# Turning the second product of a fused attention and GELU feed-forward kernel: w_out as the weights, the GELU halves as the moving side

## The chip, the cores and the metric

The kernel runs on one core of a Trainium2 chip. The metric is the device time of one execution in microseconds, as the median of repeated runs; less is better.

## What is computed

A gated linear attention (4 sequences, 8 heads, 768 steps, head size 48) whose output, 3,072 tokens by 384 columns, goes through a feed-forward layer with GELU:

```python
for t in range(S):
    state = alpha[:, :, t, :, None] * state + np.einsum('bhd,bhe->bhde', k[:, :, t], v[:, :, t])
    y[:, :, t] = np.einsum('bhd,bhde->bhe', q[:, :, t], state)
x = y.transpose(0, 2, 1, 3).reshape(B * S, H * D)          # 3072 x 384
h = x @ w_in                                               # 384 x 2048
g = 0.5 * h * (1.0 + erf(h * inv_sqrt2))
return (g @ w_out).astype(np.float32)                      # 2048 x 384
```

## The kernel before

**Work and tiles.** The tokens are cut into 12 groups of 256 (G), the 2,048 inner columns into 8 pairs of 128 (f). Both products are made of three matmuls in place of one: each operand is split into a high and a low half, and high x high, high x low and low x high are added in PSUM. A *step* is one pair of g and f, and there are 96.

**First product** (`gemm1`, L565 to L579). For each of the two blocks of a pair and each of three blocks of 128 rows it runs three matmuls: weights are a 128 x 128 block of w_in (`wih`, `wih`, `wil`), the moving side is 256 tokens of x (high, low, high). That is 18 matmuls of 256 columns into a tile `hp` of 512 columns.

**GELU.** ACT reads `hp` twice (L592, L593): once to a rounded high half `ghi`, once in place. DVE subtracts to the low half `glo` (L598). Each half is a tile of 2 x 256 columns, and two of each take turns.

**Second product** (`gemm2`, L614 to L624). For each of two blocks of 128 tokens the weights are a 128 x 128 block of a GELU half, and the moving side is a 384-column row block of w_out (`woh`, `wol`). Eight matmuls take `ghi`, then four take `glo`: 12 of 384 columns into two accumulators of 128 x 384, each in a PSUM bank of its own. The accumulators are kept while a group goes on through f, and then copied out (`evacuate`, L630 to L644): added to or copied into the tile `part` by DVE (L634, L638) or ACT (L636), the accumulators one after the other. When all of w_out has been added, POOL issues the DMA that stores `part` (L644); for the last group SP and ACT issue one DMA for each half (L640).

**Order.** A planner lays all work out before it is written down, with a table of costs (`COST`) and rules of readiness, and the order on PE, DVE, ACT and SP is then fixed by hand. After a group's x is ready PE alternates between first and second product; the second product of a step comes after the first product of the next. In between PE makes *visits* to the attention part: small tiles of 64 x 64 and 48 x 64 (L398, L425, L324, L486). In 18 visits of the later part a memset on POOL (L833, the *fence*) stands between the two halves of a visit: it waits for the matmuls before it, and the matmuls of L486 wait for it. It goes through the same queue as the output's DMA of L644.

**Places in SBUF.** Tiles are laid one behind another in their pools. `X_GAP`, `HI_GAP` and `LO_GAP` (L35) put unused bytes ahead of some tiles. With them all weight tiles begin 32 bytes past a multiple of 256, the x tiles 224 bytes past one, and the GELU halves 32 bytes past one.

Of the kernel before, what the change touches and what calls it, by code (L numbers as in the profile page):

```python
# [8 lines left out]
F32 = mybir.dt.float32  # L9
# [6 lines left out]
ALU = mybir.AluOpType  # L16
# [15 lines left out]
RATE, ALONE, LATENCY, SMALL, BEGIN = 350e3, 290e3, 2.1, 50e3, 2.2  # L32
MARGIN = 1.5
HOME = {0: 0, 1: 1, 2: 2, 4: 1, 5: 0, 6: 2, 8: 1, 9: 0, 10: 2, "s": 1}
X_GAP, Z_GAP, HI_GAP, LO_GAP, LATE_GAP = (128, 0, 192), 0, (64, 0), (0, 64), 0  # L35
COST = dict(
    scan=0.65, back=0.72, keys=0.65, q=1.35, qv=0.62, scores=1.0, kn=0.5, mask=0.62, inside=1.05, chain=1.15, outer=0.85, carry=0.26, last=0.34, last_p=0.15, sums=0.55, scaled=0.45,
    xh=0.6, xl=0.65, spread=0.62, check=0.95, load=0.46, fetch=0.46, u=0.92, c0=0.56, c1=0.9, c2=0.45, c3=0.95, c4=0.92,
# [6 lines left out]
def gla_then_gelu_ffn(ctx: ExitStack, tc: tile.TileContext, q, k, v, alpha, akq, w_in, w_out, out):  # L45
    nc = tc.nc
    B, H, D, S = q.shape
    NF, P, NK, _ = w_in.shape
    DM, DFF = NK * P, NF * P
    NT = B * S  # L50
    C = 128
    G = 2 * C
# [8 lines left out]
    NG = B * GPB  # L61
    NSB = GPB
# [4 lines left out]
    const = ctx.enter_context(tc.tile_pool(name="const", bufs=1))  # L67
# [5 lines left out]
    ps_o = ctx.enter_context(tc.tile_pool(name="ps_o", bufs=1, space=PSUM))  # L73
# [429 lines left out]
    def x_tiles(g):  # L503
        if g != "s" and g % (XB + 1) == XB:
            x = late[0].tile([P, NK, 2, G], F32R, tag="xl", name=f"x{g}")
            if g == XB:
                gap(late[0], LATE_GAP, "gap_late")
        else:
            if g in range(XB):
                gap(ffn, X_GAP[HOME[g]], f"gap_x{g}")  # L510
            x = ffn.tile([P, NK, 2, G], F32R, tag=f"x{HOME[g]}", bufs=1, name=f"x{g}")
        xt[g] = x[:, :, 0], x[:, :, 1]
        return x
# [76 lines left out]
    def gelus(g, f, hp):  # L590
        ghi = half_tile("ghi", HI_GAP, g, f)
        nc.scalar.activation(ghi, hp, AF.Gelu)  # L592
        nc.scalar.activation(hp, hp, AF.Gelu)  # L593
        return ghi
# [13 lines left out]

        return out

    parts = [const.tile([P, 2, DM], F32, name=f"part{i}") for i in range(NSB)]
    started = set()

    def gemm2(g, f, ghi, glo, acc, first, last, done, n0=None):  # L614
        for k in range(2):
            for t in range(2):
                for j in range(2):
                    for a, w in (((ghi, wo_hi[f]), (ghi, wo_lo[f])), ((glo, wo_hi[f]),))[k]:
                        nc.tensor.matmul(  # L619
                            acc[t],  # L620
                            lhsT=a[:, j, t * C : (t + 1) * C],
                            rhs=w[:, j, :],
                            start=(first and j == 0 and k == 0 and w is wo_hi[f]),
                            stop=(last and j == 1 and k == 1),  # L624
                        )
        EARLY = tuple(range(NSB))
        if not last:
            return

        def evacuate():  # L630
            o = parts[0 if g == "s" else g % NSB]
            for t in range(2):
                if g in started:
                    nc.vector.tensor_tensor(out=o[:, t], in0=o[:, t], in1=acc[t], op=ALU.add)  # L634
                elif g in EARLY or t == 1 and g == NG - 1:
                    nc.scalar.copy(o[:, t], acc[t])  # L636
                else:
                    nc.vector.tensor_copy(o[:, t], acc[t])  # L638
                if g == NG - 1:
                    (nc.scalar if t else nc.sync).dma_start(out[g * G + t * C : g * G + (t + 1) * C, :], o[:, t])  # L640
            started.add(g)
            if done and g != NG - 1:
                rows = out[g * G : (g + 1) * G, :] if n0 is None else out[bass.ds(n0, G), :]
                nc.gpsimd.dma_start(rows.rearrange("(t p) e -> p t e", p=C), o)  # L644

        return evacuate

    def general_path():
        T = 16
# [6 lines left out]
        st = flat[0][0][:, : DS * D].rearrange("p (d e) -> p d e", e=D)  # L656
# [13 lines left out]
        with tc.For_i(0, S, T) as t0:  # L670
# [21 lines left out]
            for i in range(2):  # L692
# [3 lines left out]
                    lhsT=sel,  # L696
                    rhs=yc.rearrange("p t e -> p (t e)")[:, i * half : (i + 1) * half],
                    start=True,
                    stop=True,
# [8 lines left out]
        with tc.For_i(0, NT, G) as n0:  # L708
            x_tiles("s")
            xhi, xlo = xt["s"]  # L710
            for c in range(2):
                y, z = flat[0][c][:, :DM], flat[1][c][:, :DM].rearrange("p (c h d) -> p c h d", c=NK, h=2)
                nc.sync.dma_start(y, out[bass.ds(n0 + c * C, C), :])
                main, rest = y[:, : NK * DD], y[:, NK * DD :]
                nc.vector.tensor_copy(z[..., :D], main.rearrange("p (c h d) -> p c h d", c=NK, h=2))
                nc.vector.tensor_copy(z[..., D:], rest.rearrange("p (h c d) -> p c h d", c=NK, h=2))
                xp = small_bank([P, NK, C], f"xp_s{c}")
                for i in range(NK):
                    nc.tensor.transpose(out=xp[:, i, :], in_=z[:, i].rearrange("p h d -> p (h d)"), identity=ident)
                e = slice(c * C, (c + 1) * C)  # L720
                nc.scalar.copy(xhi[:, :, e], xp)
                nc.vector.tensor_tensor(out=xlo[:, :, e], in0=xp, in1=xhi[:, :, e].bitcast(F32), op=ALU.subtract)
            acc = [ps_o.tile([P, DM], F32, tag=f"acc{t}", name=f"acc{t}_s") for t in range(2)]
            for f in range(NF2):
                hp = gemm1("s", f)
                gh = gelus("s", f, hp)
                gl = gelu_low("s", f, hp, gh)
                evacuate = gemm2("s", f, gh, gl, acc, f == 0, f == NF2 - 1, f == NF2 - 1, n0)
            evacuate()
# [224 lines left out]
    def gemm1_op(g, t):  # L954
        f = next_f[g]
        next_f[g] += 1
        st = dict(g=g, f=f, first=g != state["g"], last=False)
        prev = steps[-1] if steps else None
        if st["first"]:
            if prev:  # L960
                prev["last"] = True
                again = prev["g"] >= NSB or prev["g"] in evacuated
                evacuated.add(prev["g"])
                prev["evac"] = Op("DVE" if again else "ACT", "part", lambda p=prev: p["out"](), [prev["gemm2"]], rank=-2)
                waiting[prev["evac"].eng].append(prev["evac"])
            state["run"] += 1
        state["g"] = g
        two = steps[-2] if len(steps) > 1 else {}
        st["gemm1"] = Op("PE", "gemm1", lambda: st.update(hp=gemm1(g, f)))
        st["gelu"] = Op("ACT", "gelu", lambda: st.update(gh=gelus(g, f, st["hp"])), [st["gemm1"], two.get("gemm2")], rank=-3)  # L970
        st["gelu"].cost *= 2
        st["low"] = Op("DVE", "low", lambda: st.update(gl=gelu_low(g, f, st["hp"], st["gh"])), [st["gelu"], two.get("gemm2")], rank=-3)

        if g < NSB and t < UNTIL:
            st["minus"] = Op("PE", "minus", lambda: st.update(rest=gelu_rest(g, f, st["hp"], st["gh"])), [st["gelu"]], rank=-3)
            st["low"] = Op("ACT", "gelu", lambda: st.update(gl=st["rest"]()), [st["minus"], two.get("gemm2")], rank=-2.9)
            waiting["PE"].append(st["minus"])

        def second():
            if st["first"]:  # L980
                st["acc"] = [ps_o.tile([P, DM], F32, tag=f"acc{t}", name=f"acc{t}_{g}_{f}") for t in range(2)]
            else:
                st["acc"] = prev["acc"]
            st["out"] = gemm2(g, f, st["gh"], st["gl"], st["acc"], st["first"], st["last"], f == NF2 - 1)

        st["gemm2"] = Op("PE", "gemm2", second, [st["low"], prev and prev["gemm2"], prev and prev.get("evac")], rank=0)
        waiting["ACT"].append(st["gelu"])
        waiting[st["low"].eng].append(st["low"])
        gemms[g, f] = st["gemm1"]
        steps.append(st)  # L990
        return st["gemm1"]
# [49 lines left out]
    t = 0.0  # L1041
    idle = 0
    while True:
        moved = False
        for e in ("DVE", "ACT", "PE", "SP", "POOL"):
            if free_at[e] <= t + 1e-9:
                o = choose(e, t)
# [11 lines left out]
    last = steps[-1]  # L1059
# [90 lines left out]
```

## Time and profile before

| what | value |
|---|---|
| device time, median of 3 runs | 505.7 us (505.67 to 505.8) |
| span of the profiled execution | 505.0 us |
| median of the runs less that span | 0.7 us |
| PE busy | 489.1 us (97%) |
| weight loads busy | 475.9 us (94%) |
| DVE, ACT, POOL busy | 300.8, 219.1, 43.8 us |
| mean granted clock of TensorE | 0.996 |

The profile gives the span of the execution that was recorded, not its device time; the difference of 0.7 us to the median is what lies around the span. Busy time of PE is made of matmuls that overlap in the pipeline, so the distance from one start to the next says more than the duration of one. PEld is the load of weights, which runs beside the matmul ahead of it. A row of a timeline gives the start, the time covered, and how many instructions were merged; in brackets the idle time ahead of it, with what ended that. The granted clock is a share of 2.4 GHz.

### The profile page before, as it was taken

The numbers are of one execution on the slowest core, as the hardware profiler recorded it, in microseconds if no ns is written. First come the engines' busy times: TensorE is split into PE (matmuls) and PEld (weight loads), VectorE is DVE, ScalarE is ACT, GpSimd is POOL, SyncE is SP. The second block draws the span as 40 slices with busy tenths as digits, with TensorE's granted clock in tenths as the row PEclk, the third lists the DMA queues.
The fourth block names the chain that finished last, engine by engine and source line by source line (L and its number), as shares of the span: only waits on it lengthen the run. The fifth ranks groups of instructions, "written<-read, shape, count | busy, mean of one in ns | idle before, by whom it ended". The sixth has DMA issues, their size and how long they took to land.

```text
span 505.0 us, 13838 instructions
## 1 busy us (share of the span) xinstructions
PE 489.1 (97%) x5970; PEld 475.9 (94%) x5970; DVE 300.8 (60%) x579; ACT 219.1 (43%) x468; POOL 43.8 (9%) x80
## 2 busy tenths in 40 slices
PE   8898999999999999999999999999989999999995
PEld 8777899999999999998999999999989999999995
DVE  6999999999789999898366263251231211211211
ACT  2676856645445556554352352342322222222221
POOL 4100011000122121311020020000000000000000
PEclk9998999999999999999999999999999999999999
DMA  8956363531034454434030020010010000000001
GB/s 300 393 172 227 133 235 127 187 127 64 0 121 122 138 161 140 120 126 139 1 111 33 3 81 1 0 51 0 1 48 1 1 32 1 33 0 1 32 1 35
DMA packets 15249, 44.20 MB, mean 88 GB/s; under 512 B 2224, under 2 KB 5728, under 8 KB 15184
## 3 DMA queue, kind: packets, MB, share of 16 engines
q1 hardware_dynamic: 13520, 38.44, 23.0%
q0 software_dynamic: 1232, 4.33, 2.4%
q8 instruction: 49, 0.80, 0.7%
q10 hardware_dynamic: 432, 0.49, 0.4%
q14 instruction: 16, 0.13, 0.1%
HBM read 36.18 MB, written 4.72 MB: 81 GB/s over the span
## 4 chain that ended last, share of the span: by engine, by line
PE 78%; issue 9%; DVE 7%; ACT 3%; ACTq 1%; DMA 1%; POOL 0%; SPq 0%; DVEq 0%; POOLq 0%
PE acc L619 34%; PE hp L571 34%; PE ybank L486 3%; PE s L324 2%; PE ybank L398 1%; DVE pp L282 1%; PE ybank L425 1%; DVE rp L303 1%; ACTq L563 1%; DMA akq<-in_akq_dram 1%; DVE x L544 1%; DVE akq L308 1%; PE spare L1067 1%; DVE part L638 1%; PE ybank L366 1%
## 5 line engine op out<-in xcount | busy, mean ns | idle before, releaser
L571 PE MATMUL hp<-x,wih 128*128 128x256 f32 x1152 | 202.4, 278 | 0.0
L571 PEld LDWEIGHTS hp<-x,wih 128*128 128x128 f32 x1152 | 179.3, 189 | 0.6
L571 PE MATMUL hp<-x,wil 128*128 128x256 f32 x576 | 159.9, 278 | 0.0
L598 DVE TENSOR_TENSOR glo<-hp,ghi 128x512 fp32r<-128x512 f32 x92 | 63.0, 685 | 160.2 <-ACT hp L593 160.2
L592 ACT ACTIVATE ghi<-hp 128x512 fp32r<-128x512 f32 x96 | 57.3, 597 | 194.2 <-PE hp L571 194.1
L619 PE MATMUL acc<-woh,ghi 128*128 128x384 f32 x384 | 130.8, 341 | 0.0
L619 PE MATMUL acc<-wol,ghi 128*128 128x384 f32 x384 | 128.9, 336 | 0.0
L571 PEld LDWEIGHTS hp<-x,wil 128*128 128x128 f32 x576 | 108.9, 189 | 0.0
L619 PE MATMUL acc<-woh,glo 128*128 128x384 f32 x384 | 82.3, 335 | 1.0 <-DVE glo L598 1.0
L619 PEld LDWEIGHTS acc<-woh,ghi 128*128 128x128 f32 x384 | 72.0, 188 | 1.6
L619 PEld LDWEIGHTS acc<-wol,ghi 128*128 128x128 f32 x384 | 72.1, 188 | 0.0
L619 PEld LDWEIGHTS acc<-woh,glo 128*128 128x128 f32 x384 | 67.8, 188 | 1.6 <-DVE glo L598 1.3
L593 ACT ACTIVATE hp<-hp 128x512 f32<-128x512 f32 x96 | 57.0, 593 | 0.0
L303 DVE TENSOR_TENSOR_SCAN rp<-akq,rp,top 128x255 f32<-128x255 f32 x48 | 34.8, 753 | 0.8
L282 DVE TENSOR_TENSOR_SCAN pp<-akq,top 128x256 f32<-128x256 f32 x48 | 30.9, 677 | 3.9 <-POOL qk L298 2.0
L298 POOL TENSOR_TENSOR qk<-akq,pp 128x512 f32<-128x512 f32 x18 | 25.2, 1397 | 44.9 <-DVE pp L282 15.7
L644 POOL DMA_DIRECT2D out_dram<-part x11 | 8.3, 759 | 223.0 <-DVE part L638 209.2
L324 PE MATMUL s<-qk,akq 48*64 48x112 f32 x768 | 24.7, 260 | 1.2 <-issue 0.7
L540 ACT CAST x<-ybank 64x256 fp32r<-64x256 f32 (+4 forms) x60 | 19.9, 332 | 9.9 <-PE ybank L486 5.5
L333 ACT COPY kn<-s 128x384 f32<-128x384 f32 x24 | 11.5, 480 | 27.9 <-DVE ss L339 16.3
L453 DVE TENSOR_TENSOR states<-ybank,states 128x96 f32<-128x96 f32 x66 | 16.8, 255 | 10.3 <-ACT x L540 8.3
L308 DVE TENSOR_TENSOR akq<-akq,rp 128x512 f32<-128x512 f32 x24 | 22.3, 928 | 0.7
(79 smaller groups left out, 412.2 us busy)
## 6 DMA issues: line engine op xcount, KB each, us to landing
akq<-in_akq_dram SPq DMA_DIRECT2D x22, 768.0 KB, 5.4
st<-in_moe_w_in_dram SPq DMA_DIRECT2D x8, 768.0 KB, 4.3
st<-in_moe_w_out_dram SPq DMA_DIRECT2D x8, 768.0 KB, 4.8
vn<-in_v_dram SPq DMA_DIRECT2D x12, 384.0 KB, 4.0
out_dram<-part POOLq DMA_DIRECT2D x11, 384.0 KB, 3.8
x<-z SPq DMA_DIRECT2D x63, 32.0 KB, 1.9
akq<-in_akq_dram SPq DMA_DIRECT2D x2, 512.0 KB, 4.9
akq<-in_akq_dram SPq DMA_DIRECT2D x2, 256.0 KB, 4.0
```

The lines of the kernel that those rows point to most:

```text
L282: nc.vector.tensor_tensor_scan(pp[:, i], at[:, i], top, MID, ALU.mult, ALU.min)
L298: eng.tensor_tensor(out=qs[:, :, :, :CS], in0=by_chunk(qt), in1=by_chunk(pp), op=ALU.mult)
L303: nc.vector.tensor_tensor_scan(rp[:, i, G - 2 :: -1], at[:, i, G - 1 : 0 : -1], top[:, 1:], rp[:, i, G - 1 :], ALU.mult, ALU.min)
L308: nc.vector.tensor_tensor(out=kt, in0=kt, in1=rp, op=ALU.mult)
L324: nc.tensor.matmul(d["s"][o, h, e : e + KW], lhsT=d["kt"][r, i, t], rhs=d["qs"][r, i, j], start=True, stop=True)
L453: d["chain"] = nc.vector.tensor_tensor(out=st[j + 1], in0=new, in1=st[j], op=ALU.add)
L540: nc.scalar.copy(hi, y)
L571: nc.tensor.matmul(hp[:, j, :], lhsT=a[:, j, i * P : (i + 1) * P], rhs=x[:, i, :], start=(j == 0 and i == 0 and n == 0), stop=(i == NK - 1 ...
L592: nc.scalar.activation(ghi, hp, AF.Gelu)
L593: nc.scalar.activation(hp, hp, AF.Gelu)
L598: nc.vector.tensor_tensor(out=glo, in0=hp, in1=ghi.bitcast(F32), op=ALU.subtract)
L619: nc.tensor.matmul(acc[t], lhsT=a[:, j, t * C : (t + 1) * C], rhs=w[:, j, :], start=(first and j == 0 and k == 0 and w is wo_hi[f]), stop= ...
```

## The change

The second product is turned. A 128 x 128 block of w_out becomes the weights, and a GELU half of 256 columns is the moving side. The result stands transposed in PSUM: output columns on the partitions, tokens along the row. A step has 18 matmuls of 256 columns in place of 12 of 384. The output has three blocks of 128 columns, and `BLOCKS` puts two of them in the first accumulator (512 columns) and one in the second (256), so copies are of 512 and 256 columns in place of 384 and 384. The `part` tiles keep their size. The store writes 256 words at a time instead of 384, and the host swaps the axes back. The gaps are set so that the GELU halves begin 224 bytes past a multiple of 256, which is 192 past the weights; the x tiles stay at 224. The slow path for inputs out of range (`general_path`) makes its accumulators the same way. The planner's costs are as they were.

```diff
-X_GAP, Z_GAP, HI_GAP, LO_GAP, LATE_GAP = (128, 0, 192), 0, (64, 0), (0, 64), 0
+X_GAP, Z_GAP, HI_GAP, LO_GAP, LATE_GAP = (128, 0, 0), 0, (0, 0), (0, 0), 0
...
-    parts = [const.tile([P, 2, DM], F32, name=f"part{i}") for i in range(NSB)]
+    parts = [const.tile([P, NK, G], F32, name=f"part{i}") for i in range(NSB)]
     started = set()
+    BLOCKS = ((0, 0, 2), (1, 2, 3))
+
+    def accumulators(name):
+        return [ps_o.tile([P, i1 - i0, G], F32, tag=f"acc{b}", name=f"acc{b}_{name}") for b, i0, i1 in BLOCKS]
...
         for k in range(2):
-            for t in range(2):
-                for j in range(2):
-                    for a, w in (((ghi, wo_hi[f]), (ghi, wo_lo[f])), ((glo, wo_hi[f]),))[k]:
-                        nc.tensor.matmul(
-                            acc[t],
-                            lhsT=a[:, j, t * C : (t + 1) * C],
-                            rhs=w[:, j, :],
...
+            for b, i0, i1 in BLOCKS:
+                for i in range(i0, i1):
+                    for j in range(2):
+                        for a, w in (((ghi, wo_hi[f]), (ghi, wo_lo[f])), ((glo, wo_hi[f]),))[k]:
+                            nc.tensor.matmul(
+                                acc[b][:, i - i0],
+                                lhsT=w[:, j, i * P : (i + 1) * P],
+                                rhs=a[:, j, :],
...
-                elif g in EARLY or t == 1 and g == NG - 1:
-                    nc.scalar.copy(o[:, t], acc[t])
+                elif g in EARLY or b == 1 and g == NG - 1:
+                    nc.scalar.copy(to, acc[b])
...
-                    (nc.scalar if t else nc.sync).dma_start(out[g * G + t * C : g * G + (t + 1) * C, :], o[:, t])
+                    (nc.scalar if b else nc.sync).dma_start(turned(out[g * G : (g + 1) * G, :])[:, i0:i1], to)
...
-                nc.gpsimd.dma_start(rows.rearrange("(t p) e -> p t e", p=C), o)
+                nc.gpsimd.dma_start(turned(rows), o)
...
+    def turned(rows):
+        words = rows.rearrange("t e -> (t e)")
+        return words.rearrange("(i p t) -> p i t", p=P, t=G)
```

PE around the last visit of the attention part, before: the end of a group (`glo`), the visit (L398, L486), and the first step of the next group.

```order
L619 MATMUL acc_7_0_4774<-woh_160,glo_7_5108 128x384 x2
L619 MATMUL acc_7_0_4775<-woh_160,glo_7_5108 128x384 x2
L398 MATMUL ybank<-ss_1_4798,vn_117 64x64 x16
L486 MATMUL ybank<-qk_1848,states_131 48x64 x16
L619 MATMUL acc_8_0_5185<-woh_153,ghi_0_5144 128x384
L619 MATMUL acc_8_0_5185<-wol_161,ghi_0_5144 128x384
```

The same place after:

```order
L624 MATMUL acc_7_0_5107<-glo_7_5483,woh_160 128x256 x4
L624 MATMUL acc_7_0_5108<-glo_7_5483,woh_160 128x256 x2
L398 MATMUL ybank<-ss_1_5137,vn_117 64x64 x16
L486 MATMUL ybank<-qk_1959,states_131 48x64 x16
L624 MATMUL acc_8_0_5566<-ghi_0_5525,woh_153 128x256
L624 MATMUL acc_8_0_5566<-ghi_0_5525,wol_161 128x256
```

Nothing moved against its neighbours; the second product's matmuls are more and narrower, and the first accumulator is complete two of them before the end, as before.

POOL in the later part, before: the output's DMAs, the fences, and the products of q with the decay (L298).

```order
L298 TENSOR_TENSOR qk_120<-akq_118,pp_0_3425 128x8x64
L644 DMA out_dram<-part_173 128x2x384
L833 MEMSET done 128x1
L298 TENSOR_TENSOR qk_1848<-akq_116,pp_0_3562 128x8x64
L833 MEMSET done 128x1
```

The same place after:

```order
L298 TENSOR_TENSOR qk_120<-akq_118,pp_1_3632 128x8x64
L651 DMA out_dram<-part_173 128x3x256
L844 MEMSET done 128x1
L298 TENSOR_TENSOR qk_1959<-akq_116,pp_0_3775 128x8x64
L844 MEMSET done 128x1
```

The DMA keeps its place ahead of the fence, and its shape is now 128 x 3 x 256.

## Rows read from the trace of the kernel before

**Rows 1.** The page, section 1: busy us (share of the span) xinstructions.

```profile
PE 489.1 (97%) x5970; PEld 475.9 (94%) x5970; DVE 300.8 (60%) x579; ACT 219.1 (43%) x468; POOL 43.8 (9%) x80
```

**Rows 2.** By stretch: length; PE, PEld, DVE, ACT, POOL busy; clock; DMA; GB/s.

```profile
0.00:75.00 75.00, 67.49 (x1060) 61.31 (x1064) 67.20 (x109) 45.99 (x96) 8.86 (x32) 0.98 0.70 246
...
140.00:370.00 230.00, 227.24 (x3415) 221.17 (x3406) 146.36 (x328) 102.25 (x246) 29.14 (x41) 1.00 0.25 76
370.00:500.00 130.00, 129.38 (x939) 129.06 (x937) 26.57 (x44) 35.02 (x67) 2.18 (x3) 1.00 0.04 12
```

**Rows 3.** Chain that ended last, 400 to 505: start us, us, what.

```profile
402.38 2.04 PE hp L571 x18
404.42 2.09 PE acc L619 x12
406.51 2.04 PE hp L571 x18
```

**Rows 4.** L619 alone by stretch: length, PE and PEld busy (x matmuls), clock.

```profile
0.00:75.50 75.50, 11.38 (x60) 10.34 (x60) 0.98 0.69 244
...
87.40:505.00 417.60, 200.86 (x1068) 182.13 (x1068) 1.00 0.18 58
```

**Rows 5.** The fence, L833: durations; who waited for it (us, times).

```profile
L833 POOL MEMSET done<- x18: 93/98/118, 140.6 to 368.3; 128x1 f32 x18
...
  PEld ybank L486: 3.0, 7
```

**Rows 6.** PE timeline, second product after a visit: start us, us, what.

```profile
263.13 0.44 PE L619 MATMUL acc<-woh,ghi 128*128 128x384 f32 x1
...
264.65 0.68 PE L619 MATMUL acc<-woh,glo 128*128 128x384 f32 x3
```

**Rows 7.** PE timeline, first product after small tiles, two places.

```profile
52.09 0.28 PE L571 MATMUL hp<-x,wil 128*128 128x256 f32 x1
...
53.85 0.28 PE L571 MATMUL hp<-x,wil 128*128 128x256 f32 x1
...
177.13 0.50 PE L571 MATMUL hp<-x,wih 128*128 128x256 f32 x2
177.47 0.28 PE L571 MATMUL hp<-x,wil 128*128 128x256 f32 x1
...
179.35 0.34 PE L619 MATMUL acc<-woh,ghi 128*128 128x384 f32 x1
```

**Rows 8.** L638, all (min/median/max ns), and the page's group of L598.

```profile
L638 DVE COPY part<-acc x17: 531/547/558, 209.4 to 499.1; 128x384 f32<-128x384 f32 x17
...
L598 DVE TENSOR_TENSOR glo<-hp,ghi 128x512 fp32r<-128x512 f32 x92 | 63.0, 685 | 160.2 <-ACT hp L593 160.2
```

**Rows 9.** Timeline of a visit with the output's DMA ahead of its fence.

```profile
251.61 1.02 DVE L638 COPY part<-acc 128x384 f32<-128x384 f32 x2
...
252.93 0.75 POOL L644 DMA_DIRECT2D out_dram<-part  x1 [21.74 <-DVE part L638]
...
253.68 0.12 POOL L833 MEMSET done<- 128x1 f32 x1
...
253.85 0.67 PE L486 MATMUL ybank<-qk,states 48*48 48x64 f32 x32
```

**Rows 10.** PE timeline, the wait for the low half.

```profile
232.39 0.44 PE L619 MATMUL acc<-woh,glo 128*128 128x384 f32 x1 [1.02 <-DVE glo L598]
```

**Rows 11.** Timeline, the last two stores (DMA issues of SP and ACT).

```profile
499.65 0.35 SPq L640 DMA_DIRECT2D out_dram<-part  x1
499.93 0.39 ACTq L640 DMA_DIRECT2D out_dram<-part  x1
```

**Rows 12.** PE timeline, first product after the wait of rows 10.

```profile
233.43 0.28 PE L571 MATMUL hp<-x,wil 128*128 128x256 f32 x1
...
233.79 0.28 PE L571 MATMUL hp<-x,wil 128*128 128x256 f32 x1
233.90 0.28 PE L571 MATMUL hp<-x,wih 128*128 128x256 f32 x1
```

More of the change, by code (lines that the diff above doesn't have):

```diff
@@ L609, in gelu_rest @@
         return out
-    parts = [const.tile([P, 2, DM], F32, name=f"part{i}") for i in range(NSB)]
+    parts = [const.tile([P, NK, G], F32, name=f"part{i}") for i in range(NSB)]
     started = set()
+    BLOCKS = ((0, 0, 2), (1, 2, 3))
+    def accumulators(name):
+        return [ps_o.tile([P, i1 - i0, G], F32, tag=f"acc{b}", name=f"acc{b}_{name}") for b, i0, i1 in BLOCKS]
     def gemm2(g, f, ghi, glo, acc, first, last, done, n0=None):
         for k in range(2):
-            for t in range(2):
-                for j in range(2):
-                    for a, w in (((ghi, wo_hi[f]), (ghi, wo_lo[f])), ((glo, wo_hi[f]),))[k]:
-                        nc.tensor.matmul(
-                            acc[t],
-                            lhsT=a[:, j, t * C : (t + 1) * C],
-                            rhs=w[:, j, :],
-                            start=(first and j == 0 and k == 0 and w is wo_hi[f]),
-                            stop=(last and j == 1 and k == 1),
-                        )
+            for b, i0, i1 in BLOCKS:
[6 more added lines that the diff above has]
+                                rhs=a[:, j, :],
+                                start=(first and i == i0 and j == 0 and k == 0 and w is wo_hi[f]),
+                                stop=(last and j == 1 and k == 1),
+                                skip_group_check=True,
+                            )
         EARLY = tuple(range(NSB))
@@ L631, in evacuate @@
             o = parts[0 if g == "s" else g % NSB]
-            for t in range(2):
+            for b, i0, i1 in BLOCKS:
+                to = o[:, i0:i1]
                 if g in started:
-                    nc.vector.tensor_tensor(out=o[:, t], in0=o[:, t], in1=acc[t], op=ALU.add)
-                elif g in EARLY or t == 1 and g == NG - 1:
-                    nc.scalar.copy(o[:, t], acc[t])
+                    nc.vector.tensor_tensor(out=to, in0=to, in1=acc[b], op=ALU.add)
+                elif g in EARLY or b == 1 and g == NG - 1:
+                    nc.scalar.copy(to, acc[b])
                 else:
-                    nc.vector.tensor_copy(o[:, t], acc[t])
+                    nc.vector.tensor_copy(to, acc[b])
                 if g == NG - 1:
-                    (nc.scalar if t else nc.sync).dma_start(out[g * G + t * C : g * G + (t + 1) * C, :], o[:, t])
+                    (nc.scalar if b else nc.sync).dma_start(turned(out[g * G : (g + 1) * G, :])[:, i0:i1], to)
             started.add(g)
@@ L722, in general_path @@
                 nc.vector.tensor_tensor(out=xlo[:, :, e], in0=xp, in1=xhi[:, :, e].bitcast(F32), op=ALU.subtract)
-            acc = [ps_o.tile([P, DM], F32, tag=f"acc{t}", name=f"acc{t}_s") for t in range(2)]
+            acc = accumulators("s")
             for f in range(NF2):
@@ L980, in second @@
             if st["first"]:
-                st["acc"] = [ps_o.tile([P, DM], F32, tag=f"acc{t}", name=f"acc{t}_{g}_{f}") for t in range(2)]
+                st["acc"] = accumulators(f"{g}_{f}")
             else:
@@ L1148 @@
     got = tuple(r.results[0][f"out_{i}_dram"] for i in range(len(_OUTS)))
-    return got[0]
+    n, e = got[0].shape
+    return _np.ascontiguousarray(got[0].reshape(n // 256, e, 256).swapaxes(1, 2).reshape(n, e))
```

## The prediction, made before the changed kernel was run

> **What bounds the kernel now.** I read the busy line of the page first, then the busy time by stretch, then the chain that ended last, and last single PE rows at three kinds of place: steady, after another kind of matmul, and around a visit of the attention part. PE is busy 97% of the span [rows 1], but that is an average: up to 75 us it is busy 67.5 of 75 and DVE 67.2, in 140 to 370 it is busy 227.2 of 230, and from 370 on 129.4 of 130 with DVE at 26.6 [rows 2]. So from about 75 us on PE alone sets the end, and every nanosecond between two of its matmuls counts; before that only part of it does.
>
> What PE does there is two kinds of step in turn. In the chain, 18 matmuls of the first product take 2.04 us and 12 of the second 2.09 us [rows 3]. That is 2.04/18 = 0.1133 us for 256 moving columns and 2.09/12 = 0.174 us for 384. At the full clock of these stretches (granted 1.00 in [rows 2], the level of 2.4 GHz) 256 columns are 0.1067 and 384 are 0.160 us. The first product pays 0.0066 us per matmul beyond its columns, the second 0.014. Both move the same columns per step, 4,608, so the change is about that extra.
>
> **The change part by part.** Of the 96 steps, 1068/12 = 89 start after 87.4 us, 2 between 75.5 and 87.4, and 60/12 = 5 before [rows 4]. I count 91.
>
> *The turned matmuls in a steady step.* Removed: 12 at 0.174 = 2.087 us (406.51 - 402.38 = 4.13 for both kinds, less 2.04). Added: 18 of 256 columns. They have the first product's shape, and its place in SBUF: the program puts every weight tile 32 bytes past a multiple of 256, the x tiles 224, and the GELU halves 32 before and 224 after, which is the 192 bytes between operands that the first product has already. Price: 0.1133 each, 18 x 0.1133 = 2.040, **0.047 us less per step**. No row shows a 256-column matmul at this clock steadily under 0.113, so I take no larger gain. From above: if the extra belongs to the operands (w_out with GELU) and not to the shape, it is 0.1067 + 0.0133 = 0.120 each, 2.16 us, 0.073 more per step. I take the first, because shape and place are those of its rows; the second is a rival.
>
> [...]
>
> *The step after a restart.* PE leaves the stream for small tiles 18 times (the memset of the fence, x18 [rows 5]); 17 of these end in a step of the second product, and one at 87.4 us follows scores: 18 restarts after 75 us. Before, such a step takes 1.52 us for its first eight matmuls [rows 6] and 4 x 0.173 for the rest, 2.21 us. What a 256-column stream does after a restart is seen in the first product: at 177.13 its first two matmuls take 0.34, so the first 0.22, and from the third on 16 take 179.35 - 177.47 = 1.88 us, 0.1178 each; the same earlier (53.85 - 52.09 = 1.76 for 15, 0.117), and in all 5 runs of the first product that begin after small tiles, to their last matmul [rows 7]. So 256 columns have **two rates**, 0.1133 when entered from the 384-column stream and 0.1178 after a restart. Price of a turned step after a restart: 0.22 + 17 x 0.1178 = 2.22, 0.01 more than now; with the good rate at once, 0.22 + 17 x 0.1133 = 2.15, 0.06 less. I take the first. How long the poor rate lasts is the open question of this prediction: for the forecast I let it end with its step, where the operands change.
>
> Sum on PE: 73 x -0.047 + 18 x 0.01 = -3.4 + 0.2 = **-3.2 us** (with the good rate everywhere -3.4 - 1.1 = -4.5).
>
> *Evacuation.* 384 + 384 columns become 512 + 256. A DVE copy of 384 takes 0.547 [rows 8], an operation on 512 columns of PSUM 0.685 [rows 8], so 1.08 ns a column, 256 at 0.41; the pair stays 1.09. But the first half is now complete two matmuls of 0.1133 before the end, not two of 0.1733: the pair starts and ends 0.12 us later against PE's end. In most steps the next product's 2.04 us covers that. It is uncovered where the output's DMA on POOL stands ahead of the fence. At 251 the copies begin at 251.61, the DMA at 252.93 takes 0.75, the fence follows at 253.68 and only then PE's next matmuls at 253.85 [rows 9]. PE's weight loads were held by the fence 7 times, 3.0 us in all [rows 5]; of the eleven DMAs, eight stand ahead of a fence in POOL's order, and at six of them, as here, the fence follows without a pause. Four of the six copies find DVE free and get 0.12, two wait for DVE anyway and get about 0.04: 0.6 us.
>
> *The DMA itself.* Its rows become 384 of 1,024 bytes instead of 256 of 1,536. The trace has one shape, 0.75 us. Bounds: nothing, if it is a fixed cost; in proportion 0.75 x 1.5 = 1.12, 0.37 more; less than nothing is excluded, since the bytes stay and the rows grow. Six times 0 to 0.37 is 0 to 2.2 us; I take 0.1 each, nearer the fixed end, 0.6 us. The Trainium skill ("DMA: Bandwidth & Descriptors", section Anatomy of one DMA) calls descriptor generation small, with many descriptors before a cost shows; by it this term is 0 and the sum 0.6 less; no row here shows a second size. Together with the copies: **+1.2 us** (0.6 to 2.8).
>
> *At nothing.* The order of work on every engine stays, apart from the matmuls themselves. The 5 early steps save 0.2 us where DVE is as busy as PE; not counted. The one long wait for the low half, 1.02 us idle at 232.39 [rows 10], ends by DVE and stays. At the end the ACT half shrinks from 384 to 256 columns and its DMA, the later one at 499.93 [rows 11], comes 0.1 earlier; DVE's half grows to 512, and its DMA, now at 499.65, comes 0.12 + 0.14 later, about level. Nothing, with 0.1 either way.
>
> Sum: 505.0 span - 3.2 + 1.2 = 503.0; the runs' median lies 0.7 above the profiled span, so **503.7 us**.
>
> **The rivals.** *The poor rate lasts (slower).* What ended it in every run of [rows 7] was another shape, the 384-column stream or small tiles; after the change both products are alike in shape and place, and nothing is left that ends it. Entered at 87.4 us or at any visit, it would hold to the end: 36 x 0.1178 = 4.24 us a step against 4.13, 0.11 x 89 = 9.8, with the 1.2 above 505.7 + 11.0 = **516.7 us**. For it: five runs kept it through 17 matmuls, across changes of weight tile and of moving half. Against it: at 233.2, entered from a disturbed 384-column step, three matmuls from 233.43 took 0.36 and the next 0.11: the stream left the poor rate by itself [rows 12]. It decides from about 30 of 89 steps spent at the poor rate; a few steps after each visit would give 505 to 512.
>
> *The extra belongs to the operands.* 0.120 each, 0.073 x 91 = 6.6, with 1.2: 513.5 us. Against it: the shape and place of the first product.
>
> *Nothing gained.* The poor rate for one or two more steps after each visit (18 x 0.16 to 0.32 = 3 to 6 us) eats the gain, 505 to 507; or the DMA at its upper price, 505.3.
>
> **How the numbers follow.** A measurement of this kernel tells some 0.2%, 1 us, from no change. Forecast, from 501.6 (505.7 - 4.5 + 0.6, and the early steps' 0.2) to 504.7: 0.50. Poor rate to the end, 515 to 517: 0.30. Operands' extra, 513 to 514: 0.05. Poor rate for part of the stretches or a dear DMA, 504.7 to 513: 0.15, of which 0.08 within 0.2%. So faster 0.50, same 0.08, slower 0.42. Both signs hold much, so the forecast's own range is 501.6 to 504.7, and the range that holds 8 in 10 must reach the second case: 501.6 to 516.9.
>
> **What would show it.** Right: 18 turned matmuls in 2.04 us in the steady part after 370, first-product steps still 2.04, fences behind the DMA 0.1 to 0.3 us later. The slower rival: both kinds of step at 2.12 us after the last visit at 369, for 130 us. The operands' extra: 2.16 for the second product with 2.04 for the first. The forecast would also be wrong if the POOL row grows past 1.1 us or if PE waits for the low half more than once.

## The result: 513.7 us, slower by 1.4%

The changed kernel takes 513.73 us (median of four runs: 514.82, 513.92, 507.28 and 513.54) against 505.75 of the kernel before beside it: a ratio of 1.0136, with a 95% interval of 1.0106 to 1.0167. Three runs lie within 1.3 us of each other and one lies 6 us below them. That spread is part of the answer.

The busy line of the page after, which answers [rows 1], and two stretches, which answer [rows 2] (length; PE, PEld, DVE, ACT, POOL busy; clock; DMA; GB/s):

```profile
PE 497.4 (97%) x6546; PEld 485.6 (95%) x6546; DVE 302.7 (59%) x579; ACT 219.0 (43%) x468; POOL 45.0 (9%) x80
```

```profile
0.00:75.00 75.00, 68.79 (x1066) 63.18 (x1067) 65.34 (x106) 45.80 (x95) 9.43 (x32) 0.91 0.68 242
...
370.00:500.00 130.00, 128.56 (x1146) 128.22 (x1144) 26.57 (x44) 34.19 (x66) 3.16 (x5) 1.00 0.05 15
```

PE is busy 8.3 us longer and the span of the profiled execution is 8.2 us longer (513.2 against 505.0): PE still sets the end, and its matmuls themselves take longer. The first stretch shows that a part of this profiled run is not from the two products: its granted clock is 0.91 there, 0.98 before. That dip differs from run to run, in the kernel before too; the comparisons below therefore begin behind it.

Where the rest went stands in the chain that ended last (start us, us, what; `hp` is the first product, `acc` the second). Two pieces near 278 us, and two near 400 us, of the same run:

```profile
277.53 2.04 PE hp L571 x18
279.57 2.04 PE acc L624 x18
...
399.23 2.12 PE hp L571 x18
401.35 2.12 PE acc L624 x18
```

Against [rows 3], the turned second product takes the forecast 2.04 us for its 18 matmuls at one place and 2.12 at another: 0.1133 and 0.1178 each, the two rates that the prediction names, called good and poor below. The first product, which the change does not touch, does exactly the same: 2.04 here, 2.12 there. Following the time from one matmul's start to the next through the whole trace, a stretch between two visits of the attention part holds one rate, for both products, from about its fifth matmul on: 89 to 142 us poor, 233 to 255 good, 267 to 293 good, 305 to 332 poor, 344 to 370 good, and from the last visit to the end, 130 us, poor. It changes inside a stretch only where the stream stumbles: at 216 us two starts stand 0.18 us apart, and the poor rate turns good.

### The profile page after: what moved, and what is told of

Read it like the earlier page. It is cut to its first block, busy times and chain, and to the rows that moved or that the text cites. A ratio compares the mean times of both kernels' runs of the same rounds, so it can differ in the third digit from the quotient of the medians.

```text
span 513.2 us, 14990 instructions
## 1 busy us (share of the span) xinstructions
PE 497.4 (97%) x6546; PEld 485.6 (95%) x6546; DVE 302.7 (59%) x579; ACT 219.0 (43%) x468; POOL 45.0 (9%) x80
## 4 chain that ended last, share of the span: by engine, by line
PE 82%; issue 8%; DVE 5%; ACT 2%; DMA 1%; POOL 0%; ACTq 0%; SPq 0%; DVEq 0%; POOLq 0%
PE hp L571 35%; PE acc L624 35%; PE s L324 3%; PE ybank L486 3%; PE ybank L398 2%; PE ybank L425 2%; PE ybank L366 1%; PE spare L1078 1%; DVE pp L282 1%; DVE rp L303 1%; DMA akq<-in_akq_dram 1%; DVE x L544 1%; DVE part L645 1%; PE ybank L549 0%; DVE glo L598 0%
## 5 line engine op out<-in xcount | busy, mean ns | idle before, releaser
L571 PE MATMUL hp<-x,wih 128*128 128x256 f32 x1152 | 207.1, 281 | 0.0
L571 PEld LDWEIGHTS hp<-x,wih 128*128 128x128 f32 x1152 | 176.7, 190 | 0.6
L571 PE MATMUL hp<-x,wil 128*128 128x256 f32 x576 | 161.7, 281 | 0.0
L598 DVE TENSOR_TENSOR glo<-hp,ghi 128x512 fp32r<-128x512 f32 x92 | 63.1, 686 | 163.8 <-ACT hp L593 163.6
L624 PE MATMUL acc<-ghi,woh 128*128 128x256 f32 x576 | 140.7, 283 | 0.0
L624 PE MATMUL acc<-ghi,wol 128*128 128x256 f32 x576 | 138.4, 279 | 0.0
L624 PEld LDWEIGHTS acc<-ghi,woh 128*128 128x128 f32 x576 | 108.6, 189 | 1.6
L624 PEld LDWEIGHTS acc<-ghi,wol 128*128 128x128 f32 x576 | 108.7, 189 | 0.0
L624 PE MATMUL acc<-glo,woh 128*128 128x256 f32 x576 | 82.8, 280 | 1.1 <-DVE glo L598 1.1
L624 PEld LDWEIGHTS acc<-glo,woh 128*128 128x128 f32 x576 | 73.9, 189 | 1.2 <-DVE glo L598 1.2
L298 POOL TENSOR_TENSOR qk<-akq,pp 128x512 f32<-128x512 f32 x18 | 25.2, 1400 | 46.3 <-DVE pp L282 17.0
```

The source lines that it names most:

```text
L298: eng.tensor_tensor(out=qs[:, :, :, :CS], in0=by_chunk(qt), in1=by_chunk(pp), op=ALU.mult)
L571: nc.tensor.matmul(hp[:, j, :], lhsT=a[:, j, i * P : (i + 1) * P], rhs=x[:, i, :], start=(j == 0 and i == 0 and n == 0), stop=(i == NK - 1 ...
L598: nc.vector.tensor_tensor(out=glo, in0=hp, in1=ghi.bitcast(F32), op=ALU.subtract)
L624: nc.tensor.matmul(acc[b][:, i - i0], lhsT=w[:, j, i * P : (i + 1) * P], rhs=a[:, j, :], start=(first and i == i0 and j == 0 and k == 0 an ...
```

## The experiments

The *distance* below is the start address of the moving tile less that of the weights, in bytes, modulo 256: 192 for both products after, 192 for the first and 0 for the second before.

A window that can be compared in all traces runs from the second product that starts at 85 to 89 us (24 matmuls of 384 columns or 36 of 256 behind the scores) to the start of the last low half of the last step. Its two ends, in the PE timelines before and after:

```profile
87.58 0.44 PE L619 MATMUL acc<-woh,ghi 128*128 128x384 f32 x1
...
498.52 0.86 PE L619 MATMUL acc<-woh,glo 128*128 128x384 f32 x4
```

```profile
89.28 0.39 PE L624 MATMUL acc<-ghi,woh 128*128 128x256 f32 x1
...
506.48 0.87 PE L624 MATMUL acc<-glo,woh 128*128 128x256 f32 x6
```

This window takes 410.9 us before and 417.2 after, and with the change it starts 1.7 us later. The poor matmuls counted below are those of 256 columns in it, up to the last matmul, whose start stands 116 to 119 ns behind the one ahead: 2,142 of 3,168 after, 23 before.

### The changed kernel once more

No edit.

> The changed kernel once more, unchanged, for a second trace. Theory A: which stretches between visits run at 0.118 and which at 0.113 is drawn anew in each execution, so other stretches are poor than in the first trace, each stretch is wholly of one rate after its first few matmuls, and the time lies between 502 (all good) and 516 (all poor). Rival C (the rate is fixed by the program, by its order or its places): the same stretches are poor and the time is within 1 us of 513.7.

Measured: 507.55 us (507.42 to 509.66), a ratio of 1.0059 (1.0036 to 1.0081). The same program lies 6 us below its first result. The ends of the window, and the chain at 272 and at 400 us:

```profile
85.95 0.38 PE L624 MATMUL acc<-ghi,woh 128*128 128x256 f32 x1
...
498.89 0.84 PE L624 MATMUL acc<-glo,woh 128*128 128x256 f32 x6
```

```profile
272.19 2.12 PE acc L624 x18
274.31 2.12 PE hp L571 x18
...
401.81 2.04 PE acc L624 x18
403.85 2.04 PE hp L571 x18
```

The window takes 412.9 us with 1,176 poor matmuls. Against the first trace that is 4.3 us less for 966 fewer poor ones, 4.4 ns each, which is 117.8 - 113.3. The stretch from 263 to 291 us, good in the first trace (267 to 293), is poor here, and the last one is good. So the rate is settled at each restart, and not by the program alone. It is not wholly free either: of the 19 stretches between visits from 85 us on, 14 have the same rate in both traces, the first nine among them (86 to 139 us is poor in both); the two that stumble, at 216 and here at 212 us, change opposite ways. So the theory is right that a stretch can come out otherwise, and wrong that each is drawn anew; the rival is wrong that the program fixes all of them. The long last stretch alone, 63 products at 0.08 us, is worth 5 us. That fits three runs near 514 and one at 507, of which one at 514.82 was profiled, and it means that 1.4% and 0.6% are two samples of one kernel whose eight runs lie between 507.3 and 514.8 us.

### The place of the GELU halves alone

```diff
-X_GAP, Z_GAP, HI_GAP, LO_GAP, LATE_GAP = (128, 0, 192), 0, (64, 0), (0, 64), 0
+X_GAP, Z_GAP, HI_GAP, LO_GAP, LATE_GAP = (128, 0, 0), 0, (0, 0), (0, 0), 0
```

> The kernel before (second product not turned), with the GELU halves at 192 bytes (mod 256) from the weights as in the changed kernel; only the line of the gaps is taken over. Theory A (two rates of a 256-column stream, chosen at a restart and kept while the stream has one shape and one place): the first product is entered from the 384-column stream as before, so it stays at 0.113 us per matmul, save the one run after a visit at 0.118; time 505 to 508, depending on what 384 columns cost at 192 bytes. Rival B (the place of the GELU halves itself costs the time): 511 us or more, with the second product above 0.18 us per matmul.

Measured: 511.55 us (511.42 to 511.81), a ratio of 1.0124 (1.0107 to 1.0141). The chain:

```profile
401.43 2.12 PE hp L571 x18
403.54 2.09 PE acc L619 x12
```

The moved operands, those of the second product, cost nothing: 2.09 us as in [rows 3]. The first product pays, whose operands have not moved: 0.1178 in nearly every step. In this kernel the 384-column stream at 192 bytes hands over to it in the poor rate, the same stream at distance 0 in the good one. The time is the rival's (511 or more), the reason is neither's: the theory had the first product stay good, the rival had the second above 0.18 us per matmul.

### The turn alone

```diff
-X_GAP, Z_GAP, HI_GAP, LO_GAP, LATE_GAP = (128, 0, 0), 0, (0, 0), (0, 0), 0
+X_GAP, Z_GAP, HI_GAP, LO_GAP, LATE_GAP = (128, 0, 192), 0, (64, 0), (0, 64), 0
```

> The changed kernel with the gaps of the kernel before: second product turned, GELU halves at 0 bytes (mod 256) from the weights, x at 192. Theory A: the two products now differ in place, so a poor rate entered after a visit need not survive the change from one product to the other; no stretch between visits has both products at 0.118 to its end, and the time depends on the rate of 256 columns at 0 bytes: 0.113 gives 503, 0.118 gives 508, 0.120 gives 510. Rival B (turning costs the time, whatever the place): 512 to 515, with both products at 0.118 in the last 130 us.

Measured: 513.46 us (512.48 to 514.61), a ratio of 1.0168 (1.0147 to 1.019). The chain:

```profile
402.10 2.06 PE hp L571 x18
404.16 2.14 PE acc L624 x18
```

At distance 0 the turned product runs at 0.119 to 0.120 per matmul in the steady steps, and each step of it leaves the first product at the good rate (2.06: three or four slower matmuls at the entry, then 0.1133). As the theory had it, no stretch keeps both products at 0.118; its 510 us for a rate of 0.120 was too low, and the rival's 512 to 515 holds the time without its reason. Each half of the change is slower alone, by 6 and 8 us, in another product each.

### The distance alone

Only matmuls; the attention, the feed-forward and the output are left out. Behind small tiles comes a stream of 36 matmuls of 256 columns, four times for each moving tile, each tile 32 bytes further from the weights; then 12 matmuls of 384 columns and 24 of 256 straight behind them.

```diff
+    for w, ms in ((wa, moving), (wb, moving[::2])):
+        for m in ms:
+            for n in SMALL:
+                small(n)
+                after_small(w, m, STREAM)
+            small(32)
+            wide(w, m, WIDE)
+            after_wide(w, m, 24)
```

> Only matmuls, no attention and no feed-forward; the output is zeros. Streams of 36 matmuls of 256 columns, each after 16 to 40 small tiles of 48 x 64, with the moving tile at 0, 32, ... 224 bytes (mod 256) from the weights, four streams for each; then 12 matmuls of 384 columns after small tiles and 24 of 256 straight behind them. A last set has the weights 64 bytes further on. Theory A: at 192 bytes streams after small tiles run at 0.118 or 0.113, those behind the 384 columns at 0.113; other distances have other rates, and at least one keeps a single rate however it is entered. Rival B (a plain cost of the place): one rate for each distance, the same after small tiles and behind 384 columns. If the absolute place counts and not the distance, the last set differs from the first at the same distance.

The PE timeline (start us, us from the first start to the last end). Tiles ma to mh stand 0, 32, ... 224 bytes (mod 256) from the weights wa; from wb, which lie 64 bytes elsewhere, ma stands at 192 and mc at 0:

```profile
21.11 4.57 PE L69 MATMUL hp<-ma,wa 128*128 128x256 f32 x36
...
46.99 4.47 PE L69 MATMUL hp<-mb,wa 128*128 128x256 f32 x36
...
109.95 4.57 PE L69 MATMUL hp<-md,wa 128*128 128x256 f32 x36
...
147.81 4.53 PE L69 MATMUL hp<-me,wa 128*128 128x256 f32 x36
...
173.60 4.49 PE L69 MATMUL hp<-mf,wa 128*128 128x256 f32 x36
179.50 4.54 PE L69 MATMUL hp<-mf,wa 128*128 128x256 f32 x36
...
205.25 4.51 PE L69 MATMUL hp<-mg,wa 128*128 128x256 f32 x36
...
211.17 4.37 PE L69 MATMUL hp<-mg,wa 128*128 128x256 f32 x36
...
232.62 2.99 PE L73 MATMUL hp<-mg,wa 128*128 128x256 f32 x24
...
268.21 4.37 PE L69 MATMUL hp<-ma,wb 128*128 128x256 f32 x36
...
273.98 4.50 PE L69 MATMUL hp<-ma,wb 128*128 128x256 f32 x36
...
295.55 2.89 PE L73 MATMUL hp<-ma,wb 128*128 128x256 f32 x24
...
299.39 4.57 PE L69 MATMUL hp<-mc,wb 128*128 128x256 f32 x36
```

A row of 36 holds 0.22 for the first start, 34 distances and 0.28 for the last, so 4.37 is 0.1138 with its entry, 4.51 is 0.118 and 4.57 is 0.120. Seven of the eight distances never give less than 4.47. Only 192 gives 4.37, and it gives two values far apart: in turn, two of four each, for ma from wb as for mg from wa. Two other distances also show two values, closer together: 160 (4.49 and 4.54) and, from wb, 128 (4.54 and 4.59). At the four distances taken from both weight tiles the values agree to 0.05 us, so what counts here is the distance, not the place; and 192, the best of all, is the one where the two rates matter. Straight behind 384 columns at 192 the stream ran once poor (2.99 for 24 from wa) and once good (2.89 from wb): the poor handover of the run before is not a rule, and the theory's good one came once of two.

### What brings the good rate

Only matmuls again. The stream at 192 bytes (mg) is entered in seven ways, eight times each: directly behind small tiles, behind 1, 2, 3 or 6 matmuls of 256 columns at distance 0 (ma), and behind 1 or 2 of 384 columns there:

```diff
+    for n in range(8):
+        for stream in (direct, narrow1, narrow2, narrow3, narrow6, wide1, wide2):
+            small(17 + 3 * n)
+            stream()
```

> Only matrix products of one loaded tile, and zeros written to the output: all the rest of the computation is left out. After a run of small tiles (17 to 38 of them, eight lengths) comes a stream of 36 products of 256 columns whose moving tile stands 192 bytes (mod 256) from the weights, entered in seven ways, eight times each: directly; behind 1, 2, 3 or 6 products of 256 columns at distance 0; behind 1 or 2 products of 384 columns at distance 0. Theory (at the entry the stream falls by chance into one of two rates, 113.3 or 117.8 ns, and keeps it; coming from a stream at distance 0 it falls into the good one): direct 3 to 5 of 8 at 113.3 ns, the rest at 117.8; behind 6 at distance 0 8 of 8 at 113.3; behind 1 to 3 it is open how many are enough. Rival (the good rate in the changed kernel comes from something else, what came before the visit or the data): the kinds do not differ, each 3 to 5 of 8.

```profile
49.74 4.37 PE L69 MATMUL hp<-mg,wa 128*128 128x256 f32 x36
...
72.78 0.98 PE L91 MATMUL hp<-ma,wa 128*128 128x256 f32 x6
73.60 4.26 PE L93 MATMUL hp<-mg,wa 128*128 128x256 f32 x36
...
85.22 4.40 PE L105 MATMUL hp<-mg,wa 128*128 128x256 f32 x36
...
177.34 4.51 PE L69 MATMUL hp<-mg,wa 128*128 128x256 f32 x36
```

Behind another stream the first start takes 0.12, so good is 4.26 there and poor 4.40. Good, of eight: direct 6 (the first of them took 0.213 us a matmul in its first half and settled at the good rate behind it); behind 1, 2 or 3 matmuls at distance 0: 6, 6 and 4; behind 6: 8; behind one of 384 columns: 8; behind two: 2. Direct entries were expected good 3 to 5 times and were so 6 times; six at distance 0 always did it, as expected, and the rival, by which the ways would not differ, falls. That two wide ones do worse than one was not expected. It may be the moment at which the stream is entered that counts, not a rest or a shape; no run here shows it.

### A reset in every second step

One of the two tiles for low halves moved to distance 0, so that the last 6 of 18 turned matmuls of every second step stand there. Such a run of matmuls at distance 0 is called a *reset* below:

```diff
-X_GAP, Z_GAP, HI_GAP, LO_GAP, LATE_GAP = (128, 0, 0), 0, (0, 0), (0, 0), 0
+X_GAP, Z_GAP, HI_GAP, LO_GAP, LATE_GAP = (128, 0, 0), 0, (0, 0), (0, 64), 0
```

> The changed kernel with one of its two tiles of GELU low halves moved by 64 bytes, to distance 0 from the weights; the two tiles take turns by the step, so in every second step the last 6 of the 18 products of the second GEMM run at distance 0. Theory (a stream at distance 0 brings the good rate back): those 6 take some 120 ns each, and whatever rate a stretch was entered at, behind the first such step all runs at 113.3 ns; no stretch of poor steps longer than two; 45 x 6 x 6.7 ns = 1.8 us for the slower products against 10 to 40 steps rid of 0.16 us each; 504 to 507 us, the runs within 1 us of each other. Rival 1 (the rate is set by the entry behind a visit alone): long poor stretches stay, 507 to 515 us, the runs apart by several us. Rival 2 (the change of distance is itself an entry that draws anew): good and poor steps alternate inside one long stretch, half of all poor, 508 to 511 us.

Measured: 505.28 us (503.90 to 507.02), a ratio of 0.999 (0.9971 to 1.0009). It is no longer told apart from the kernel before: a move of 64 bytes takes the loss away. The chain:

```profile
407.54 2.06 PE acc L624 x18
409.61 2.06 PE hp L571 x18
411.66 2.04 PE acc L624 x18
413.70 2.04 PE hp L571 x18
```

The step with the six slower matmuls takes 2.06 + 2.06, the other 2.04 + 2.04, all the way to the end; nowhere is a stretch longer than two steps poor. Of the 48 resets 41 are followed by another product without a visit between, and all 41 times it runs at the good rate, 9 times out of the poor one. The first rival (the entry alone decides) and the second (a reset draws anew) fall. Run again, beside the last kernel below, it gave 505.48 us and a ratio of 1.0002 (0.9987 to 1.0016), again with 41 of 41. The medians lie where they were expected; the runs do not lie within 1 us of each other, as was expected too: all 22 lie between 503.6 and 507.5 us, and those of the kernel before scatter as widely:

> The run with one low tile at distance 0 again, beside the other: 504.5 to 506 us; against it the one with two resets should be 0.5 to 1.5 us faster by the theory, and within 0.3 us by the rival.

### A reset behind each visit alone

A third tile for low halves at distance 0, used by the first run of the second product behind each visit:

```diff
+    def reset_tile(g, f):
+        t = late[0].tile([P, 576], F32R, tag="glr", bufs=1, name=f"glr_{g}_{f}")
+        return t[:, 16 : 16 + 2 * G].rearrange("p (j t) -> p j t", j=2)
...
-        glo = half_tile("glo", LO_GAP, g, f)
+        if (g, f) in fresh and late:
+            glo = reset_tile(g, f)
+        else:
+            glo = half_tile("glo", LO_GAP, g, f)
...
```

> The changed kernel, with a third tile for the low GELU halves at distance 0 from the weights, used only by the first second GEMM behind each of the 18 visits from 134 us on; all other steps keep the distance of 192 bytes. Theory (6 products at distance 0 bring the good rate, which then stays until the next visit): behind each such step both products run at 113.3 ns, the stretch to the end among them; against the run with one low tile moved, 45 - 18 = 27 fewer steps with 6 slow products (27 x 0.04 = 1.1 us less): 503.0 to 504.8 us, the stretch of 87 to 137 us, ahead of the first visit, still left to chance (up to 2 us). Rival 1 (the gain of that run came from the reset in every second step; a single one does not hold for a long stretch): poor stretches behind the first step, 505 to 510 us. Rival 2 (a tile elsewhere or a changed order of the low halves costs a wait of its own): 505 us or more with all products at 113.3 ns.

Measured: 505.0 us (median of twelve, 503.67 to 511.48); without the run at 511.48 the ratio is 0.9992 (0.9969 to 1.0016). The ends of the window, and one reset in the chain:

```profile
88.39 0.39 PE L632 MATMUL acc<-ghi,woh 128*128 128x256 f32 x1
...
497.43 0.84 PE L632 MATMUL acc<-glo,woh 128*128 128x256 f32 x6
```

```profile
160.01 2.38 PE acc L632 x18
162.39 4.24 PE hp L571 x36
```

The window takes 409.0 us, 1.9 less than before, with 258 poor matmuls. Of the 18 resets 17 leave the good rate behind them, nine of these out of the poor one; two stretches of 27 us (263 and 302 us) were entered poor and stay good behind their single reset to their end, so the first rival falls. Behind the last visit the rate stays good for 130 us, but there it was good before the reset; and the stretch from 88 to 140 us, which has no reset, was good by luck. The reset at 160, inside which the stream stumbled (its second matmul 0.21 us behind its first), left the next two products poor (4.24 for 36); the same stumble at 213 us did not. So six do not always do it. A reset that fails ahead of the last stretch would cost 5 us; the one run at 511.48 may be that, but there is no trace of it. The median lies 0.2 us above the 503.0 to 504.8 that the theory expected.

### Which half spoils the first product

The kernel before, with only the high halves at 192 bytes, and with only the low ones, which stand last in each step:

```diff
-X_GAP, Z_GAP, HI_GAP, LO_GAP, LATE_GAP = (128, 0, 192), 0, (64, 0), (0, 64), 0
+X_GAP, Z_GAP, HI_GAP, LO_GAP, LATE_GAP = (128, 0, 0), 0, (0, 192), (64, 64), 0
```

> The kernel before, with the two tiles of high GELU halves at 192 bytes (mod 256) from the weights and the low ones left at distance 0: the last 4 of the 12 products of 384 columns are at distance 0, the first 8 are not. Theory (what stands last ahead of the first product decides at which rate it is entered): the first product stays at 113.3 ns, 18 in 2.04 us, the second at 173.3 to 173.5; 505.0 to 506.5 us. Rival (any product of 384 columns at 192 bytes spoils the step, by its share): the first product at 117.8 ns in most steps, 508 to 511.5 us.

```diff
-X_GAP, Z_GAP, HI_GAP, LO_GAP, LATE_GAP = (128, 0, 192), 0, (64, 0), (0, 64), 0
+X_GAP, Z_GAP, HI_GAP, LO_GAP, LATE_GAP = (128, 0, 192), 0, (64, 64), (192, 0), 0
```

> The kernel before, with the two tiles of low GELU halves at 192 bytes (mod 256) from the weights and the high ones left at distance 0: the last 4 of the 12 products of 384 columns are at 192 bytes. Theory (what stands last ahead of the first product decides): the first product at 117.8 ns in nearly every step, as with all halves at 192; 510.5 to 512.5 us. Rival (by the share of the products at 192 bytes, 4 of 12): 505.5 to 508 us.

Measured: 506.8 us (ratio 1.0021, 1.0001 to 1.004) with the high halves away, 513.53 (1.0146, 1.0105 to 1.0186) with the low ones. The chains, in this order:

```profile
404.10 2.10 PE acc L619 x12
406.21 2.04 PE hp L571 x18
```

```profile
404.79 2.12 PE hp L571 x18
406.91 2.11 PE acc L619 x12
```

The last four matmuls ahead of the first product decide, not the share of eight or four. Both times are above what the theory expected, by 0.3 and 1.0 us, and both chains show a new term: a second product that changes its distance on the way takes 2.10 to 2.11 instead of 2.09, 1 to 2 us over 89 steps.

### Two resets behind each visit

Distance 0 in every second step up to 137 us, then in the first and third run of the second product behind each visit, and 192 in all others (a third tile, `glk`):

```diff
+    def low_tile(g, f):
+        if not late:
+            return half_tile("glo", LO_GAP, g, f)
+        if (g, f) in fresh:
+            return ffn.tile([P, 2, G], F32R, tag="glo1", bufs=1, name=f"glo_{g}_{f}")
...
```

> The changed kernel with low GELU halves at distance 0 only where they are to bring the good rate back: in every second step up to 137 us, and from there on in the first and third second GEMM behind each visit; a third tile for low halves, at 192 bytes, takes the place of the one at distance 0 in all other steps. Theory: as with one reset behind each visit (505.0 us median, best 503.7), without its two leaks, a stretch ahead of 137 us left to chance and a reset that fails behind a stall: every long stretch at 113.3 ns, some 25 of the 45 slow second GEMMs of the run with one low tile gone (25 x 0.04 = 1.0 us): 503.2 to 505.0 us, without runs above 508. Rival (what is left above 504 us is not the rate but the evacuation and the waits of the visits, which no reset touches): 505 to 506 us with every long stretch at 113.3 ns.

```profile
86.78 0.38 PE L635 MATMUL acc<-ghi,woh 128*128 128x256 f32 x1
...
496.31 0.84 PE L635 MATMUL acc<-glk,woh 128*128 128x256 f32 x6
```

Measured: 504.37 us (503.54 to 506.57) against 505.51, a ratio of 0.9992 (0.9977 to 1.0007): no difference that these runs can tell. The window takes 409.5 us, 1.4 less than before, without a stretch that stays poor. Beside the kernel with one low tile, run with it (505.48), the median is 1.1 us lower, where the theory had 0.5 to 1.5; the means are 0.7 apart, with 12 runs each that scatter over 3 to 4 us, so this is not settled. None of the twelve runs is above 506.6, but the kernel before had none above 507.5 in the same set either. What is left of the gain is about the size of the scatter that the start brings. No version here is shown to beat the kernel before.

## Why the prediction was wrong

**What bounds the kernel**: right. PE's busy time grew by 8.3 us and the span by 8.2.

**The turned matmuls in a steady step**: right at the good rate, 2.04 as forecast. The rival price of 0.120 is real too, but belongs to distance 0 (the turn alone), not to w_out and GELU as operands. Matmuls of one shape took 0.1133, 0.1178 and 0.120 here, for 0.1067 us of columns, so no fixed extra describes them.

**The step after a restart**: half right. It is entered at either rate, not always at the poor one.

**The step that failed** is this one: "How long the poor rate lasts is the open question of this prediction: for the forecast I let it end with its step, where the operands change". It does not end there. A change of operands at the same distance keeps it; in the runs here only matmuls at distance 0, a stumble of the stream or a new restart ended it. Where a step of the second product followed the runs of [rows 7], its 384 columns at distance 0 were the cure, not the end of the step. The change took the cure out of every step: 2,142 poor matmuls in the window where the forecast had 18 x 18 = 324, (2142 - 324) x 4.4 ns = 8.0 us. With the 1.7 us by which the window starts later, in part the dip of the clock in this one run, 503.0 + 8.0 + 1.7 = 512.7, against the profiled span of 513.2.

**Evacuation and DMA**: forecast +1.2 us. Of the fence, who waited for it (us, times; [rows 5] has 3.0, 7), and the output's DMA on POOL (min/median/max ns):

```profile
  PEld ybank L486: 4.0, 7
```

```profile
L651 POOL DMA_DIRECT2D out_dram<-part x11: 762/807/1007, 150.6 to 476.7; - x11
```

The fence holds PE's weight loads 1.0 us more; PE itself waits for it 1.2 us more (2.6, 6 against 1.4, 2), in part the same time. That fits the forecast. The DMA of 384 rows instead of 256 takes 0.81 us on POOL instead of 0.75, 0.06 more where I took 0.1 and the upper bound was 0.37. The Trainium skill ("DMA: Bandwidth & Descriptors", section Anatomy of one DMA) calls the generation of descriptors small; the trace agrees, with these 0.06 us for half as many rows again.

**The sum** was therefore about right for what it described, -3.2 + 1.2 = -2.0 us: the line through the two traces of the changed kernel (417.2 us at 2,142 poor matmuls, 412.9 at 1,176) gives 409.2 at the forecast's 324, 1.7 below the kernel before, and the run with a reset behind each visit, where the poor rate mostly ends with its step, is 1.9 below it in the window.

**The rivals.** *The poor rate lasts* named the mechanism, its price and its sign; it had the stretches all poor, 516.7, where each takes one rate or the other. What I held against it, [rows 12], was misread: the stream there did not leave the poor rate by itself. It came out of a second product at distance 0, and three or four slow starts stand ahead of the good rate at other entries too (117, 117, 123 and 118 ns in the stream at 211.17 of the matmuls alone, then 113). Its turning point was put at 30 of 89 steps; the same line meets 410.9 at about 720 matmuls, 20 steps. *The extra belongs to the operands* had 513 to 514 us, where the first median lies: that is luck, since both products took 2.04 or 2.12 us and the second never 2.16. What came is the case given 0.15, the poor rate for part of the stretches; its upper end of 513 was too low, and the second set, 507.55, lies inside it. The median also lies inside the wide range of 501.6 to 516.9, which was drawn to hold the poor rate as well. The chance of 0.50 for the forecast was too high: with nothing in view that would end the rate, the burden was on its ending.

**Open**: what sets the rate at an entry, and why the distance matters at all. The direct entries were in turn good and poor in one run of matmuls alone and 6 of 8 good in the other, and 14 of 19 stretches came out alike in two traces; whether it is chance or the exact moment was not settled.

## What to carry to other kernels

Where one engine's back-to-back stream bounds a kernel, measure its rate per instruction at several places of one trace, and ask of any rate that has two values what ends each. An edit that makes all streams alike removes whatever brought the better value back, so price the worse one for whole stretches. When runs of one program spread by more than a per cent, compare two traces of that same program first.

## What the runs showed of the hardware

- In the run of matmuls alone, from 20 us on, at a granted clock of 1.00, the rate of a stream of 256-column matmuls with a weight load each depends on the distance between the moving tile and the weights: 120 ns at 0, 117 at 32, 118 at 64, 120 at 96, 118 to 120 at 128, 117 to 119 at 160, 118 at 224; at 192 either 113.3 or 117.8. 384 columns take 173 to 177 ns.
- At 192 both rates sustain themselves: up to 130 us and over a thousand matmuls in the two traces of the changed kernel, across changes of weights, tile and product, but the poor one not across a run at distance 0.
- Behind small tiles, six matmuls of 256 columns, or one of 384, at distance 0 led to the good rate 8 times of 8; two of 384 only 2 of 8. Inside the kernels six at distance 0 led to it 41 times of 41, 41 of 41 and 17 of 18.
